# Fused attention and two feed-forward layers: which first-layer slices run inside attention, and how the decay table is loaded

## The chip, the cores and the metric

The kernel runs on one core of one Trainium2 chip. The metric is the device time of one execution in microseconds. The core has five engines that work from queues of their own and wait for each other by semaphores: TensorE (PE in the profile; PEld is its loading of weights), VectorE (DVE), ScalarE (ACT), GpSimd (POOL) and SyncE (SP), which here issues all DMA transfers.

## The reference

```
# q, k, v: [2 batches, 8 heads, 768 tokens, 64]; lam: one decay per head, 0.97 to 0.99
# per head, by blocks of 64 tokens:
intra = ((q_b k_b^T) * Dmask) v_b        # Dmask[i, j] = lam ** (i - j) for i >= j, else 0
inter = (q_b * lam ** (i + 1)) state
state = lam ** 64 * state + (k_b * lam ** (63 - j))^T v_b
x = heads side by side: [1536 tokens, 512]
h = x @ w_in                             # 512 -> 2048
x = act(h) @ w_out                       # act: 0 below -1, h above 1, (h + 1)**2 / 4 between
out = (sigmoid(x @ w_gate) * (x @ w_val)) @ w_out2     # 512 -> 1536 -> 512
```

## The kernel before

**Attention.** Blocks of 128 tokens are used instead of 64. There are 16 units, one for each batch, pair of heads and half of the tokens (384 tokens, three blocks). In the loop over units i, TensorE is given: the scores of unit i+1 (`scores`, L412), the state updates of unit i+1 (`updates`, L427), then the outputs of unit i (`outputs`, L475 from the weighed scores, L484 from the states). VectorE weighs the scores of i+1 with the decay table `DT` into `pT` (L442), builds the states `sc` (L451, L453), and writes the low part `xl` of unit i's output (L495); ScalarE copies the states (`st`, L465) and writes the high part `xh` (L494). GpSimd scales the keys of unit i+2 by the last column of `DT` (`pre_k`, L388, `kd`), and behind the outputs the queries of unit i+2 by the table `qp` (`pre_q`, L398, `qs`). SP loads unit i+4 into one of four buffers once unit i is done, then one weight piece.

**Numbers in two parts.** The feed-forward matmuls take each factor as a high part in the fast 32-bit format and a low part that holds the rest, so each product is three matmuls: high x high, low x high, high x low. The weights arrive as 64-bit floats in pieces of 512 columns (512 KB). A round (`w_round`) is a pipeline step over three pieces: `w_float` on piece k-1 (L92 and L93 on VectorE, L95 on VectorE or GpSimd), `w_high` on piece k-2 (L99, ScalarE), `w_words` on piece k (L85, L86, ScalarE) and `w_low` on piece k-2 (L103, the subtraction that makes the low part). Piece k-2 is usable when round k is done. Pieces 0, 1, 3, 5 are the four hidden weights of the first group, pieces 2, 4, 6, 7 their projection weights.

**Feed-forward.** `feed_forward` is a generator over (layer, group, third of the tokens, f); a group has four f. Each entry makes one hidden slice of twelve matmuls 128x512 (two slices in the second layer), then `act1` or `act2` makes `r` from it (L173, L174 on ScalarE, L175 on VectorE), and one entry later `split` makes the high part `gh` (L165, ScalarE) and low part `gl` (L166, VectorE). `finish` takes the oldest split entry and does its projection, again twelve matmuls (L202), into four accumulator banks, which are copied out behind the fourth f. PSUM has eight banks in one pool: scores (two), updates, outputs, hidden slice and the four accumulators all take theirs from it.

**What runs where.** The attention loop takes `next(steps)` at units 7 to 15 but 13. Each step is a hidden slice, or a projection, for which the generator stops a second time inside attention. The first third of the tokens (512) is complete behind unit 7, the second behind unit 14. By the code's order the eight steps are: hidden 0, 1, 2, projection 0, hidden 3, projection 1, hidden 4 (the second third), projection 2. Weight rounds stand at units 1, 3 and 5 to 12, ten of them, with L95 and L103 on GpSimd. Behind attention, `rounds` is not empty, the generator runs to its end, and rounds are done wholly on VectorE and ScalarE.

**Tables.** Ahead of unit 0, `tables` builds the first two heads' part of `DT` on VectorE and GpSimd (L346, L349), the first pair's `qp` on ScalarE (L357) and a row of powers per head, `pw`, on ScalarE (L363). `pw` is stored to memory (`pd`, L365), and two loads of `qp` (L370) and one of `DT` for heads 2 to 7 (L375, 384 KB) read it back, shifted by one element per partition.

Of the kernel before, what the change touches and what calls it, by code (L numbers as in the profile page):

```python
# [10 lines left out]
AF = mybir.ActivationFunctionType  # L11
# [3 lines left out]
B, H, S, D = 2, 8, 768, 64  # L15
NT, DM = B * S, H * D
FF1, FF2 = 2048, 1536
P = 128
# [7 lines left out]
GF = 4  # L26
PADW = 64
CST = 4 + PADW + P
FFREE = (13,)
NQD = 2  # L30
NWP, NRAW = 14, 5

# [2 lines left out]
def fused_kernel(ctx: ExitStack, tc: tile.TileContext, qkv, qd, cst, w1, w2, out):  # L35
    nc = tc.nc
    pe, act, dve, pool, sp = nc.tensor, nc.scalar, nc.vector, nc.gpsimd, nc.sync
# [63 lines left out]
    def w_low(i, eng):  # L101
        r = tmps.pop(i)[1]
        eng.tensor_tensor(out=ws[i][:, 1], in0=r, in1=ws[i][:, 0].bitcast(F32), op=ALU.subtract)  # L103

    def w_round(eng=dve, between=None):
        k = prog["round"]
        if k - 2 >= len(pieces):
            return  # L110
        if k - 2 >= NWP and pieces[k - 2 - NWP][0] >= prog["done"]:
            return
        prog["round"] += 1
        if 0 <= k - 1 < len(pieces):
            w_float(k - 1, eng)
        if between:
            between()
        if 0 <= k - 2:
            w_high(k - 2)
        if k < len(pieces):  # L120
            while prog["loaded"] <= k:
                w_load()
            w_words(k)
        if 0 <= k - 2:
            w_low(k - 2, eng)
        if eng is dve:
            w_load()

# [102 lines left out]
    def feed_forward(rounds):  # L231
        LAG = 2
        behind = []
        fresh = None

        def split():
            (ph, g, t, f), a = fresh
            behind.append((fresh[0], parts(a, ph * NF1 + g * GF + f, t)))

        def finish():  # L240
            (ph, g, t, f), gs = behind.pop(0)
            project((ph, g, t, f), gs)
            if f == GF - 1:
                flush((ph, g, t, f))
            if t == NTT - 1:
                prog["done"] += 1
            return f == GF - 1

        for u in seq:
            ph, g, t, f = u  # L250
            n = ph * NF1 + g * GF + f
            hs = [hidden(n, t, 0)] + ([hidden(n, t, 512)] if ph else [])
            if fresh:
                split()
            fresh = u, (act2(*hs, n, t) if ph else act1(hs[0], n, t))
            yield u
            flushed = False
            if len(behind) == LAG:
                flushed = finish()
                if not rounds:  # L260
                    yield u
            if rounds:
                if ph:
                    w_round()
                    w_round()
                elif not flushed:
                    w_round()
        split()
        while behind:
            finish()  # L270

    rounds = []
    steps = feed_forward(rounds)


    with ExitStack() as actx:
# [6 lines left out]
        nu = len(units)  # L283
# [30 lines left out]
        def tables():  # L314

            cs = tp.tile([P, 512], F32, tag="r", bufs=3, name="cs")
            dm = [tp.tile([P, 512], F32, tag="r", bufs=3, name=f"dm{j}")[:, 0:2 * (PADW + P)]
                  .rearrange("p (h x) -> p h x", h=2) for j in range(2)]
            sp.dma_start(out=cs[:, 0:CST], in_=cst)
            for i in range(NQD):  # L320
                u_load(i)
                q_diag[i] = wp.tile([P, 2, 512], F32, tag="w", name=f"qd{i}").rearrange(
                    "p a b -> p (a b)")[:, 0:2 * UT].rearrange("p (c e t) -> p c e t", c=CU, e=2)
                u_part(i, 1, 1)
                for c in range(CU):
                    if c < 2 or i:
                        c1 = CU if c or i else 1
                        sp.dma_start(out=q_diag[i][:, c:c1], in_=qd[i][:, c:c1])
                    if i:
                        break  # L330
            for i in range(NQD):
                u_part(i, 2, 2)
            for i in range(NQD):
                u_part(i, 0, 1)
            for j in range(2):
                dve.memset(dm[j][:, :, 0:PADW], 0.0)
            dve.memset(half, 0.5)
            pool.memset(pw[:, 0:P - 1], 0.0)
            pool.memset(pw[:, P - 1:P], 1.0)
            pool.memset(st[0], 0.0)  # L340
            act.activation(st[1], st[0], AF.Copy)
            sq = [cs[:, 0:2]] + [cs[:, CST + 2 * k:CST + 2 * k + 2] for k in range(6)]
            for k in range(7):
                w = 1 << k
                if k:
                    pool.tensor_tensor(out=sq[k], in0=sq[k - 1], in1=sq[k - 1], op=ALU.mult)  # L346
                for h in range(2):
                    src = cs[:, 4:CST] if k == 0 else dm[k % 2][:, h]
                    dve.scalar_tensor_tensor(  # L349
                        out=DT[:, h] if k == 6 else dm[(k + 1) % 2][:, h, PADW:],  # L350
                        in0=src[:, PADW - w:PADW + P - w], scalar=sq[k][:, h:h + 1],
                        in1=src[:, PADW:], op0=ALU.mult, op1=ALU.add,
                    )
            act.activation(qp[:, 0, 0:1], cs[:, 3:4], AF.Copy)
            for k in range(7):
                w = 1 << k
                act.activation(qp[:, 0, w:2 * w], qp[:, 0, 0:w], AF.Copy,  # L357
                               scale=qp[:, 0, w - 1:w])

            act.activation(pw[:, P:P + 1], cs[0:H, 2:3], AF.Copy)  # L360
            for k in range(7):
                w = 1 << k
                act.activation(pw[:, P + w:P + 2 * w], pw[:, P:P + w], AF.Copy,  # L363
                               scale=pw[:, P + w - 1:P + w])
            sp.dma_start(out=pd, in_=pw)  # L365
            u_load(2)
            w_load()
            pdv = pd[:, :]
            for e in range(2):
                sp.dma_start(  # L370
                    out=qp[e * D:(e + 1) * D, 1:],
                    in_=bass.AP(pdv.tensor, pdv.offset + (2 + e) * 2 * P + P,
                                [[0, D], [4 * P, NP - 1], [1, P]]),
                )
            sp.dma_start(  # L375
                out=DT[:, 2:],
                in_=bass.AP(pdv.tensor, pdv.offset + 4 * P, [[1, P], [2 * P, H - 2], [1, P]]),
            )
            u_load(3)
            w_load()  # L380

# [118 lines left out]
        with tc.manual_schedule():  # L500
# [11 lines left out]
            for i in range(nu):  # L512
# [9 lines left out]
                    outputs(i)  # L522
                    evacuate(i)

                if i in (1, 3) or 5 <= i <= 12:
                    w_round(pool, finish)
                else:
                    finish()
                if i + 2 < nu:
                    pre_q(i + 2)  # L530
                u_load(i + 4)
                w_load()
                if i >= nu // 2 - 1 and i not in FFREE:
                    next(steps)


# [68 lines left out]
```

## Time and profile before

| | us |
|---|---|
| median of 3 runs | 637.87 |
| lowest and highest run | 637.09, 2779.6 |
| the profiled execution, device time | 638.09 |
| its span, first to last instruction | 636.3 |
| TensorE busy in the span | 614.8 (97%) |
| VectorE, ScalarE, GpSimd busy | 352.5, 287.2, 56.8 |
| mean granted TensorE clock, of full speed | 0.983 |

The span is what the trace covers; the device time lies 1.79 us above it. Busy shares are means over the whole run: GpSimd works only in the first 90 us, and TensorE's idle time lies almost wholly there too. A bracket behind a row of a timeline gives the idle time of the engine before it and what ended it. SPq and POOLq are the queues in which SP and GpSimd issue DMAs.

### The profile page before, as it was taken

What the parts mean: (1) busy time and instruction counts of PE and PEld (TensorE: products, weight loads), DVE (VectorE), ACT (ScalarE), POOL (GpSimd) and SP (SyncE); (2) the same over time, 40 slices, a digit from 0 to 9 for tenths busy, and PEclk for the clock granted to TensorE, in tenths of its full rate; (3) what the DMA queues carried; (4) which work ended last, traced back from release to release, by engine and by line L of the source; (5) the groups of instructions that cost most, each with busy time, mean ns of one, the idle gap of its engine ahead of it and who ended that gap; (6) DMA issues with size and microseconds to landing.
All of it is one profiled execution on the core that took longest, in us unless ns stands there. A gap on an engine that the chain in (4) does not pass through costs nothing.

```text
span 636.3 us, 7871 instructions
## 1 busy us (share of the span) xinstructions
PE 614.8 (97%) x3072; PEld 507.7 (80%) x3072; DVE 352.5 (55%) x612; ACT 287.2 (45%) x511; POOL 56.8 (9%) x62
## 2 busy tenths in 40 slices
PE   6779889999999999999999999999999999999997
PEld 5667668888888888888888888888888888888886
DVE  4485864655666666666776912157843167713132
ACT  5356745665565556556675612144721145311110
POOL 3486740000000000000000000000000000000000
PEclk9789979999999999999999999999999999999999
DMA  8985520322132223122213400024420022001011
GB/s 262 349 291 220 199 66 1 101 66 67 66 100 66 67 67 91 56 60 92 66 34 99 133 0 1 1 66 133 132 67 0 1 59 74 1 1 67 0 67 66
DMA packets 16229, 53.37 MB, mean 84 GB/s; under 512 B 1720, under 2 KB 3648, under 8 KB 16192
## 3 DMA queue, kind: packets, MB, share of 16 engines
q1 hardware_dynamic: 16192, 52.87, 25.5%
q8 instruction: 24, 0.39, 0.3%
q14 instruction: 13, 0.11, 0.0%
HBM read 49.71 MB, written 3.15 MB: 83 GB/s over the span
## 4 chain that ended last, share of the span: by engine, by line
PE 88%; ACT 4%; DVE 4%; DMA 2%; issue 1%; POOL 1%; SPq 0%; POOLq 0%; ACTq 0%; DVEq 0%
PE a L202 35%; PE h L147 17%; PE h L148 17%; PE h L149 17%; DVE pT L442 1%; DMA DT<-pd 1%; PE x L484 1%; PE x L475 1%; ACT xh L494 1%; ACT st L465 1%; PE s L412 1%; DVE sc L453 1%; DMA pd<-pw 1%; DVE r L175 0%; DVE part L216 0%
## 5 line engine op out<-in xcount | busy, mean ns | idle before, releaser
L147 PE MATMUL h<-xh,w 128*128 128x512 f32 x480 | 188.3, 392 | 0.0
L148 PE MATMUL h<-xh,w 128*128 128x512 f32 x480 | 187.7, 391 | 0.0
L149 PE MATMUL h<-xl,w 128*128 128x512 f32 x480 | 187.3, 390 | 0.0
L202 PE MATMUL a<-gh,w 128*128 128x512 f32 x384 | 118.7, 390 | 0.5 <-DVE r L175 0.5
L148 PEld LDWEIGHTS h<-xh,w 128*128 128x128 f32 x480 | 90.7, 189 | 19.0 <-POOL w L103 0.3
L149 PEld LDWEIGHTS h<-xl,w 128*128 128x128 f32 x480 | 90.6, 189 | 18.9
L147 PEld LDWEIGHTS h<-xh,w 128*128 128x128 f32 x480 | 90.7, 189 | 18.6
L181 DVE TENSOR_TENSOR r<-r,h 128x512 f32<-128x512 f32 x36 | 24.7, 687 | 139.4 <-PE h L149 137.1
L202 PE MATMUL a<-w,gh 128*128 128x512 f32 x288 | 88.6, 389 | 0.0
L202 PEld LDWEIGHTS a<-gh,w 128*128 128x128 f32 x384 | 71.8, 188 | 15.5 <-DVE r L175 0.9
L175 DVE SCALAR_TENSOR_TENSOR r<-r,h 128x512 f32<-128x512 f32 x48 | 33.0, 687 | 87.1 <-ACT r L174 87.0
L165 ACT ACTIVATE gh<-r 128x512 fp32r<-128x512 f32 x84 | 52.4, 624 | 60.8 <-DVE r L181 55.5
L202 PE MATMUL a<-gl,w 128*128 128x512 f32 x192 | 74.7, 389 | 0.0
L173 ACT ACTIVATE r<-h,half 128x512 f32<-128x512 f32 x48 | 33.0, 688 | 91.5 <-PE h L149 91.5
L166 DVE TENSOR_TENSOR gl<-r,gh 128x512 fp32r<-128x512 f32 x84 | 58.4, 695 | 16.5 <-ACT gh L165 16.4
L202 PEld LDWEIGHTS a<-w,gh 128*128 128x128 f32 x288 | 54.1, 188 | 11.2
L180 ACT ACTIVATE r<-h 128x512 f32<-128x512 f32 x36 | 21.5, 597 | 87.2 <-PE h L149 87.2
L99 ACT ACTIVATE w<-wr 128x512 fp32r<-128x512 f32 x68 | 42.4, 623 | 39.6 <-DVE wr L95 39.2
L202 PE MATMUL a<-w,gl 128*128 128x512 f32 x144 | 56.0, 389 | 0.0
L93 DVE SCALAR_TENSOR_TENSOR wr<-raw,wr 128x512 uint32<-128x512 uint32 x68 | 50.1, 737 | 2.3
L85 ACT ACTIVATE wr<-raw 128x512 f32<-128x512 f32 x68 | 45.1, 664 | 0.8 <-POOL w L103 0.8
L86 ACT ACTIVATE wc<-raw 128x512 int32<-128x512 uint32 x68 | 44.8, 658 | 0.0
(51 smaller groups left out, 513.5 us busy)
## 6 DMA issues: line engine op xcount, KB each, us to landing
raw<-in_w SPq DMA_DIRECT2D x68, 512.0 KB, 3.6
u<-in_qkv SPq DMA_DIRECT2D x14, 768.0 KB, 5.7
out<-part SPq DMA_DIRECT2D x12, 256.0 KB, 2.1
u<-in_qkv SPq DMA_DIRECT2D x4, 192.0 KB, 5.6
u<-in_qkv SPq DMA_DIRECT2D x2, 384.0 KB, 6.2
qd<-in_qd SPq DMA_DIRECT2D x1, 384.0 KB, 5.4
DT<-pd SPq DMA_DIRECT2D x1, 384.0 KB, 6.3
qd<-in_qd SPq DMA_DIRECT2D x1, 256.0 KB, 3.7
```

Source lines behind the costliest of these rows:

```text
L85: act.activation(r, hi.bitcast(F32), AF.Copy, scale=2.0 ** -112)
L86: act.activation(c, lo, AF.Copy, scale=2.0 ** -29)
L93: dve.scalar_tensor_tensor(out=ru, in0=hi, scalar=0x80000000, in1=ru, op0=ALU.bitwise_and, op1=ALU.bitwise_or)
L99: act.activation(ws[i][:, 0], tmps[i][1], AF.Copy)
L147: pe.matmul(h, lhsT=wh, rhs=xh[:, k, tt], start=(k == 0), stop=False)
L148: pe.matmul(h, lhsT=wl, rhs=xh[:, k, tt], start=False, stop=False)
L149: pe.matmul(h, lhsT=wh, rhs=xl[:, k, tt], start=False, stop=(k == NP - 1))
L165: act.activation(gh, g, AF.Copy)
L166: dve.tensor_tensor(out=gl, in0=g, in1=gh.bitcast(F32), op=ALU.subtract)
L173: act.activation(r, h, AF.Relu, bias=half, scale=0.5)
L175: dve.scalar_tensor_tensor(out=r, in0=r, scalar=1.0, in1=h, op0=ALU.min, op1=ALU.max)
L202: pe.matmul(accs[j], lhsT=a, rhs=b_, start=(f == 0 and m == 0), stop=(f == GF - 1 and m == 2))
```

## The change

Four things are changed. First, inside attention only hidden slices are made, one each behind units 7, 9, 11 and 13; no projection runs there. To allow that, `finish` waits until three entries are split while attention runs (`LAG + 1`), and the generator no longer stops behind a projection. Behind attention the lag is two, as before, and a `while` does two projections at once at the first step there. Each projection is followed by its weight rounds as before. Second, the ten weight rounds stand at units 1, 3, 5, 6, 7, 8, 10, 12, 14 and 15. Third, in rounds at units below 8 the low-part subtraction (L103) runs on VectorE and no longer on GpSimd; there are three such subtractions, at units 5, 6 and 7 (the first two rounds have none). Fourth, in `tables` ScalarE makes `pw` first and stores it, then `qp`; the `DT` reload is cut into heads 2 and 3 and heads 4 to 7; the first weight load moves behind both.

```diff
--- before.py
+++ after.py
@@ -26,7 +26,8 @@
 GF = 4
 PADW = 64
 CST = 4 + PADW + P
-FFREE = (13,)
+HIDDEN = (7, 9, 11, 13)
+ROUNDS = (1, 3, 5, 6, 7, 8, 10, 12, 14, 15)
 NQD = 2
 NWP, NRAW = 14, 5
 
@@ -104,7 +105,7 @@
 
 
 
-    def w_round(eng=dve, between=None):
+    def w_round(eng=dve, between=None, low=dve):
         k = prog["round"]
         if k - 2 >= len(pieces):
             return
@@ -122,7 +123,7 @@
                 w_load()
             w_words(k)
         if 0 <= k - 2:
-            w_low(k - 2, eng)
+            w_low(k - 2, low)
         if eng is dve:
             w_load()
 
@@ -254,12 +255,8 @@
                 split()
             fresh = u, (act2(*hs, n, t) if ph else act1(hs[0], n, t))
             yield u
-            flushed = False
-            if len(behind) == LAG:
+            while len(behind) >= (LAG if rounds else LAG + 1):
                 flushed = finish()
-                if not rounds:
-                    yield u
-            if rounds:
                 if ph:
                     w_round()
                     w_round()
@@ -339,6 +336,18 @@
             pool.memset(pw[:, P - 1:P], 1.0)
             pool.memset(st[0], 0.0)
             act.activation(st[1], st[0], AF.Copy)
+
+            act.activation(pw[:, P:P + 1], cs[0:H, 2:3], AF.Copy)
+            for k in range(7):
+                w = 1 << k
+                act.activation(pw[:, P + w:P + 2 * w], pw[:, P:P + w], AF.Copy,
+                               scale=pw[:, P + w - 1:P + w])
+            sp.dma_start(out=pd, in_=pw)
+            act.activation(qp[:, 0, 0:1], cs[:, 3:4], AF.Copy)
+            for k in range(7):
+                w = 1 << k
+                act.activation(qp[:, 0, w:2 * w], qp[:, 0, 0:w], AF.Copy,
+                               scale=qp[:, 0, w - 1:w])
             sq = [cs[:, 0:2]] + [cs[:, CST + 2 * k:CST + 2 * k + 2] for k in range(6)]
             for k in range(7):
                 w = 1 << k
@@ -351,20 +360,7 @@
                         in0=src[:, PADW - w:PADW + P - w], scalar=sq[k][:, h:h + 1],
                         in1=src[:, PADW:], op0=ALU.mult, op1=ALU.add,
                     )
-            act.activation(qp[:, 0, 0:1], cs[:, 3:4], AF.Copy)
-            for k in range(7):
-                w = 1 << k
-                act.activation(qp[:, 0, w:2 * w], qp[:, 0, 0:w], AF.Copy,
-                               scale=qp[:, 0, w - 1:w])
-
-            act.activation(pw[:, P:P + 1], cs[0:H, 2:3], AF.Copy)
-            for k in range(7):
-                w = 1 << k
-                act.activation(pw[:, P + w:P + 2 * w], pw[:, P:P + w], AF.Copy,
-                               scale=pw[:, P + w - 1:P + w])
-            sp.dma_start(out=pd, in_=pw)
             u_load(2)
-            w_load()
             pdv = pd[:, :]
             for e in range(2):
                 sp.dma_start(
@@ -372,10 +368,13 @@
                     in_=bass.AP(pdv.tensor, pdv.offset + (2 + e) * 2 * P + P,
                                 [[0, D], [4 * P, NP - 1], [1, P]]),
                 )
-            sp.dma_start(
-                out=DT[:, 2:],
-                in_=bass.AP(pdv.tensor, pdv.offset + 4 * P, [[1, P], [2 * P, H - 2], [1, P]]),
-            )
+            for h0, h1 in ((2, 4), (4, H)):
+                sp.dma_start(
+                    out=DT[:, h0:h1],
+                    in_=bass.AP(pdv.tensor, pdv.offset + h0 * 2 * P,
+                                [[1, P], [2 * P, h1 - h0], [1, P]]),
+                )
+            w_load()
             u_load(3)
             w_load()
 
@@ -522,15 +521,15 @@
                     outputs(i)
                     evacuate(i)
 
-                if i in (1, 3) or 5 <= i <= 12:
-                    w_round(pool, finish)
+                if i in ROUNDS:
+                    w_round(pool, finish, pool if i >= nu // 2 else dve)
                 else:
                     finish()
                 if i + 2 < nu:
                     pre_q(i + 2)
                 u_load(i + 4)
                 w_load()
-                if i >= nu // 2 - 1 and i not in FFREE:
+                if i in HIDDEN:
                     next(steps)
```

## Rows read from the trace of the kernel before

**Rows 1.** Stretches: from:to, length, five engines' busy us (instructions), TensorE clock, DMA share, GB/s

```profile
7.50:27.50 20.00, 15.32 (x140) 12.91 (x139) 7.26 (x20) 5.45 (x14) 8.60 (x10) 0.83 0.97 342
27.50:40.00 12.50, 10.65 (x155) 8.93 (x153) 10.16 (x27) 6.87 (x16) 8.35 (x9) 1.00 0.90 307
40.00:50.00 10.00, 7.80 (x52) 6.38 (x48) 6.48 (x11) 5.72 (x12) 10.00 (x10) 0.66 0.85 304
50.00:100.00 50.00, 45.82 (x379) 36.19 (x378) 33.22 (x63) 28.29 (x55) 27.64 (x24) 0.93 0.39 138
100.00:632.00 532.00, 532.00 (x2349) 440.63 (x2347) 290.10 (x474) 234.53 (x399) 0.00 (x0) 1.00 0.18 57
```

**Rows 2.** Chain that ended last: start, length, what; one slice behind attention

```profile
101.96 2.72 PE a L202 x12
```

**Rows 3.** Timeline of TensorE in attention: start us, length, engine, line, what

```profile
50.17 0.94 PE L412 MATMUL s<-u 64*128 64x128 f32 x12
...
55.46 0.94 PE L412 MATMUL s<-u 64*128 64x128 f32 x12
...
58.17 0.47 PE L147 MATMUL h<-xh,w 128*128 128x512 f32 x1
...
96.23 0.70 PE L202 MATMUL a<-gh,w 128*128 128x512 f32 x2
```

**Rows 4.** Timeline of the first 21 us, several engines; in brackets idle time before

```profile
2.92 2.36 ACT L357 ACTIVATE qp<-qp 128x1 f32<-128x1 f32 x7
...
3.53 2.35 SPq L296 DMA_DIRECT2D u<-in_qkv  x4
...
5.41 2.35 ACT L363 ACTIVATE pw<-pw 8x1 f32<-8x1 f32 x7
...
7.84 0.34 SPq L365 DMA_DIRECT2D pd<-pw  x1
...
12.71 0.60 SPq L375 DMA_DIRECT2D DT<-pd  x1
...
19.13 0.56 DVE L442 TENSOR_TENSOR pT<-s,DT 128x384 f32<-128x384 f32 x1 [2.46 <-DMA DT<-pd]
...
20.09 0.91 PE L427 MATMUL uu<-u,kd 128*64 128x64 f32 x12 [3.99 <-POOL kd L388]
```

**Rows 5.** Timeline of 39 to 48 us, around unit 8, several engines

```profile
39.00 1.28 POOL L103 TENSOR_TENSOR w<-wr,w 128x512 fp32r<-128x512 f32 x1
...
39.58 0.94 PE L412 MATMUL s<-u 64*128 64x128 f32 x12 [0.76 <-DMA u<-in_qkv]
...
40.60 1.36 DVE L93 SCALAR_TENSOR_TENSOR wr<-raw,wr 128x512 uint32<-128x512 uint32 x1
...
42.71 0.91 PE L427 MATMUL uu<-u,kd 128*64 128x64 f32 x12 [2.20 <-POOL kd L388]
...
47.04 0.56 DVE L495 TENSOR_TENSOR xl<-x,xh 128x384 fp32r<-128x384 f32 x1 [0.24 <-ACT xh L494]
```

**Rows 6.** Chain that ended last, 58 to 66 us, steps of one unit

```profile
58.41 0.69 DVE r L175
...
61.98 0.63 ACT w L99
...
63.76 0.52 ACT gh L165
...
64.28 0.58 ACT r L173
...
65.55 0.70 DVE r L175
```

**Rows 7.** Waits of TensorE up to 120 us: total us, times, longest

```profile
PE s L412 <- DVE pT L442: 2.1, 2, 1.1
```

**Rows 8.** Groups by line: busy us, mean ns | idle before; page, first 150 us

```profile
L93 DVE SCALAR_TENSOR_TENSOR wr<-raw,wr 128x512 uint32<-128x512 uint32 x68 | 50.1, 737 | 2.3
...
L103 DVE TENSOR_TENSOR w<-wr,w 128x512 fp32r<-128x512 f32 x7 | 5.0, 709 | 0.0
```

## Prediction

> **What bounds the kernel now.** I read the table of stretches first. From 100 to 632 us TensorE is busy for 532.00 of 532 us at full clock; before that it is busy 7.80 of 10 us between 40 and 50, at a granted clock of 0.66, and 45.82 of 50 us between 50 and 100, at 0.93 [rows 1]. So nothing behind attention can be hidden or gained, and only what happens up to about 100 us is open. The chain that ended last gives the price of the unit of work: twelve matmuls of 128x512, called a slice here, take 2.72 us when TensorE runs without a gap [rows 2]. The code has 48 first-layer hidden slices, 48 first-layer projections and 36 x 3 in the second layer, 204 in all. When the last attention matmuls make room for the next projection at 96.2 us [rows 3], seven slices are done (five hidden, two projected) and 197 are left: 96.2 + 197 x 2.72 = 632.0, and the span of 636.3 leaves a tail of 4.3 (the last accumulation and stores).
>
> That gives the formula for the changed kernel. It does four hidden slices inside attention, so 200 are left. With X for the moment when TensorE has issued its last attention matmul, span = X + 200 x 2.72 + 4.3 = X + 548.3. The profiled time is 638.09 for a span of 636.3, so the time is X + 550.1. The median of the runs is 637.87, and the difference of 0.2 does not matter here. **Break-even is X = 88.0**: three slices (8.2 us) go behind attention, so attention must end 8.2 us sooner to pay for them. Every slice that TensorE takes later costs exactly what it saved, unless attention was waiting for something other than TensorE.
>
> **Part by part: the tables.** ScalarE computes the powers `pw` before `qp` instead of behind it, so `pw` is ready one chain of 2.36 us sooner than at 7.76 [rows 4]. The store `pd` can't use all of it: SP issues loads until 5.88, so the store moves from 7.84 to 5.9 at best. Its landing may not move at all, since it stands in the queue behind the same loads: bounds 0 and 1.9. The `DT` reload, issued at 12.71, was waited for until 19.13 by the first weighing of the second head pair, and through the key scaling on GpSimd by the updates at 20.09, with TensorE idle for 3.99 us [rows 4]. Now one third of it comes first, and a weight load of 512 KB no longer stands ahead. I take a landing at 15.5, between 13.4 and 19.0, nearer the early end because two thirds of the bytes and one load are out of the way. The updates then start near 16.5, about 3.5 us sooner. What moves back: `qp` is ready at 7.8 instead of 5.3, hidden because GpSimd uses it from 11.3 on; if that cover were gone it would cost 2.5. In SP's queue the load of unit 3 comes some 1.0 later, behind one more issue of 0.6 and a weight load's; the same bytes stand ahead of it, so I cost it at nothing, at most 1.0.
>
> That gain does not last. The DMA share is 0.97 between 7.5 and 27.5 and 0.90 between 27.5 and 40 [rows 1]: 0.6 + 1.25 = 1.85 us of idle transfer time in all, and every byte has still to come. At 39.58 the scores of unit 8 waited for their own load [rows 5]. So at unit 8 the tables are worth between 0 and 1.85; I take 1.0.
>
> **Units 5 to 7: three low-part subtractions from GpSimd to VectorE.** GpSimd takes 1.28 for one at 39.00, and behind it stood the key scaling for which the updates of unit 8 waited until 42.71, TensorE idle for 2.20 [rows 5]. After these idle times TensorE was granted half its clock in the stretch from 40 to 50 [rows 1]. Without the subtraction, and 1.0 sooner, the updates start at 42.7 - 1.3 - 1.0 = 40.4; 1.85 for the rest of the unit at full clock (2.71 from 55.46 to 58.17 [rows 3], less the scores) and one slice of 2.73 end at 45.0. That is TensorE's bound for the end of the first hidden slice, now just before 50.17 [rows 3]. VectorE has another: that slice's last matmul needs `xl` of unit 7, ready at 47.6 now [rows 5]. Two subtractions at 0.71 [rows 8] come before it (49.0); the shift takes 1.0, and a GpSimd that is less busy gives back about two times 0.6 (L93 took 1.36 at 40.60 against a mean of 0.74 [rows 5, 8]), and its idle time ahead of that `xl`, 0.24 and some before it, fills up. I take 45.9 for `xl` and 46.2 for the end of the slice: between 45.0 and 49.3 (no shift, nothing given back), by VectorE because it ends last. The first slice's `r` on VectorE then starts at 47.6, since relu and square take 1.4 [rows 6].
>
> **Units 8 to 15.** In the kernel before, each of units 7 to 12 had a weight round and a slice or projection. From 58.41 to 65.55 the chain goes through ScalarE and VectorE, not TensorE: 7.14 a unit, of which 1.78 is the round's work on ScalarE (L99, L85, L86) between the evacuation and the split [rows 6]. Now a unit with a slice alternates with one with a round. TensorE needs 58.17 - 50.17 = 8.00 for such a pair [rows 3]. The chain from one `r` to the next loses the 1.78 (ScalarE does it in the other unit, while VectorE weighs) and gains one unit's weighing (two at 0.56 [rows 4] and two state steps, 1.4), the round's L92 and L93 (1.15) and one `xl` (0.5): 7.14 - 1.78 + 3.05 = 8.4. I take 8.5 a pair, between 8.0 (TensorE) and 9.6 (both round operations doubled, as L93 was). So `r` of the second and third slice start at 56.1 and 64.6.
>
> The fourth slice, at unit 13, meets a new wait. Its weight piece is finished in the round of unit 12, on GpSimd. Counted from the third `r`: `r` 0.6, weighing 1.4, L92 and L93 1.15, then two GpSimd operations of 1.28 [rows 5] give 5.9 with the handover; TensorE could have started at 3.85. Everything on TensorE queues behind this second matmul of the slice. The slice ends at 8.65 and its `r` starts at 10.1 instead of 8.5: 74.7. The last weighing and the last outputs take 3.6 more (0.6, 1.4, 0.1, and 1.5 of matmuls): **X = 78.3**. Without the stall it is 76.7.
>
> The four accumulator banks that the projections held are free, so the 2.1 us in which scores waited for `pT` to release a bank [rows 7] go, with the slow clock after them. This is inside the pair count already. Behind attention two whole projections (5.4 us) cover the last evacuation and the fourth slice's split; the rounds there run with TensorE full, as now, so I cost the lag of three at nothing. If that cover failed it would show as TensorE idle behind X, at most one ScalarE-VectorE chain of some 3 us.
>
> **Sum.** 78.3 + 550.1 = 628.4 us, 9.7 below the profiled run, 1.5%.
>
> **Rivals.** A: TensorE itself is the bound of each pair and the fourth weight piece comes in time. 45.0 + 1.4 + 3 x 8.0 + 3.6 = 74.0, or 624.1; with the full 1.85 of the tables 623.3. For it: the chain of 8.4 is only just above 8.0. Against it: the piece of unit 12 has three operations in a row ahead of it. Chance 0.16.
>
> B: VectorE and GpSimd hold each other up, and the stall at the fourth slice lowers the clock. L93 went from 0.74 to 1.36 beside a working GpSimd [rows 5, 8]; three subtractions prolonged by 0.6 each give 1.8, and a slice and a unit partly at the lower of the two clock levels give 2.5, as the stretch from 40 to 50 did after idle times of the same size [rows 1, 5]. 628.4 + 1.8 to 4.3 = 630.2 to 632.7, to 634.5 with the pairs at 9.0. Chance 0.22. The Trainium skill (SBUF — State Buffer, Who interferes with whom) states the rule that speaks against the change: a VectorE instruction with two SBUF inputs and a GpSimd instruction that reads SBUF lock each other out, and the later one blocks wholly. The subtraction is of that kind; by that rule it could wait for a whole GpSimd operation. The trace's 1.36 agrees in kind.
>
> C, on the other side: the rounds and the attention chain, not the slices, set the pace, and units 8 to 15 keep their average, (96.2 - 50.2) / 8 = 5.75 us. Then X = 46.2 + 8 x 5.75 = 92.2 and the time 642.3, slower than before. It decides from 5.2 us a unit. For it: the chain ran through ScalarE and VectorE. Against it: that chain contained the 1.78 only because slice and round fell in one unit, and the bank waits belong to the projections. Chance 0.08.
>
> That the tables change does nothing at all is in the sum's bounds: 1.0 later, 629.4.
>
> **How the numbers follow.** The forecast's own range is 626 to 631, chance 0.50; A 0.16, B 0.22, C 0.08, and 0.04 lies outside them all. The range 623.5 to 634.5 holds the forecast, nearly all of B and most of A. Two per cent, about what a measurement of this kernel can tell from no change, is 12.8 us: faster means below 625.1, which is most of A (0.13); slower means above 650.6, which only several failures give (0.02); 0.85 lies between.
>
> **What would show it.** The updates of unit 2 start near 16.5, not 20.09; unit 8's scores near 38.5; no half clock between 40 and 50. The first slice ends near 46, the `r` of the four slices come 8.5 apart with a longer last step, TensorE waits about 2 us for L103 on GpSimd in the fourth slice, and the last attention matmul ends near 78. Behind it, 200 slices at 2.72 without a gap. The prediction is wrong if VectorE's chain gives pairs over 9.6, if the clock falls more than once behind 40 us, or if TensorE is idle behind X.

## The result, and the profile after

The changed kernel takes 630.57 us in the median (629.64 to 631.58, 4 runs) against 637.48 for the kernel before on the same chip: a ratio of 0.9894, 95% interval 0.9872 to 0.9917, 1.1% faster. The ratio leaves out one run of the kernel before, of 2779.6 us. The profiled execution took 631.58 us with a span of 629.8, the slowest of the four. On another occasion six runs gave 630.84 (629.05 to 631.61), ratio 0.9904.

Lines behind the changed places are shifted by up to one in the new kernel: L203 is the projection, L148 to L150 the hidden slice, L411 the scores, L426 the updates, L441 the weighing, L474 and L483 the outputs, L104 the low-part subtraction, L96 the round's addition on GpSimd, L176 the `r`.

The chain that ended last, behind attention. It answers [rows 2]; columns are start, length and what.

```profile
100.63 2.72 PE a L203 x12
```

A slice still costs 2.72 us. TensorE took up its first projection with ten of its matmuls behind the last outputs at 81.77, two of them having slipped in ahead: X = 81.3. The formula gives 81.3 + 548.3 = 629.6 for a span of 629.8. So attention ended 14.9 us sooner than 96.2 and gave 8.2 of it back as three slices.

Stretches of the changed kernel, to be laid beside [rows 1]: from:to, length, busy us of the five engines with their instructions, granted clock, DMA share, GB/s.

```profile
40.00:50.00 10.00, 6.86 (x66) 5.31 (x68) 8.57 (x17) 6.77 (x14) 7.70 (x8) 0.96 0.77 288
...
49.00:53.00 4.00, 4.00 (x40) 3.33 (x38) 2.73 (x8) 1.87 (x6) 1.73 (x2) 0.57 0.18 53
```

Between 40 and 49 there is no low clock in this execution (0.66 over 40 to 50 before). It came once, from 49 to 53, at 0.57. In the other profiled execution of the same kernel, of 630.69 us, it is the other way round: full clock from 49 to 53, and half clock from 42 to 44.

```profile
42.00:44.00 2.00, 2.00 (x16) 1.67 (x13) 1.90 (x3) 1.85 (x4) 1.66 (x2) 0.50 0.77 315
```

So the kernel does not fix where the clock falls, and the forecast of no half clock between 40 and 50 holds in one of two profiles, and there up to 49.

The start of the changed kernel, against [rows 4].

```profile
5.70 0.71 SPq L345 DMA_DIRECT2D pd<-pw  x1
...
12.05 1.33 SPq L366 DMA_DIRECT2D qp<-pd  x2
...
13.42 1.11 SPq L372 DMA_DIRECT2D DT<-pd  x2
...
18.17 0.56 DVE L441 TENSOR_TENSOR pT<-s,DT 128x384 f32<-128x384 f32 x1 [1.05 <-DMA DT<-pd]
...
19.13 0.91 PE L426 MATMUL uu<-u,kd 128*64 128x64 f32 x12 [2.50 <-POOL kd L387]
```

The store of `pw` was issued 2.1 us sooner than before (5.70 against 7.84), and what reads it back was issued 0.7 us later (12.05 against 11.33): SP waited 5.1 us for the store to land, 2.2 before. The updates of unit 2 came at 19.13, 0.96 sooner.

Units 7 and 8, against [rows 5]: scores and updates of unit 8, a subtraction of the change beside GpSimd's addition, then what the first slice waited for.

```profile
38.81 0.94 PE L411 MATMUL s<-u 64*128 64x128 f32 x12
...
41.46 0.57 PE L426 MATMUL uu<-u,kd 128*64 128x64 f32 x12 [1.71 <-POOL kd L387]
...
42.56 1.29 POOL L96 TENSOR_TENSOR wr<-wr,wc 128x512 int32<-128x512 int32 x1 [1.15 <-DVE wr L94]
...
43.01 1.39 DVE L104 TENSOR_TENSOR w<-wr,w 128x512 fp32r<-128x512 f32 x1
...
46.76 0.49 ACT L493 ACTIVATE xh<-x 128x384 fp32r<-128x384 f32 x1
...
47.31 0.50 PE L148 MATMUL h<-xh,w 128*128 128x512 f32 x1 [1.68 <-ACT xh L493]
```

The `r` operations of the four slices and the last outputs.

```profile
50.30 0.69 DVE L176 SCALAR_TENSOR_TENSOR r<-r,h 128x512 f32<-128x512 f32 x1 [1.23 <-ACT r L175]
...
59.51 0.69 DVE L176 SCALAR_TENSOR_TENSOR r<-r,h 128x512 f32<-128x512 f32 x1 [1.15 <-ACT r L175]
...
68.06 0.69 DVE L176 SCALAR_TENSOR_TENSOR r<-r,h 128x512 f32<-128x512 f32 x1 [0.46 <-ACT r L175]
...
78.04 0.69 DVE L176 SCALAR_TENSOR_TENSOR r<-r,h 128x512 f32<-128x512 f32 x1 [1.94 <-ACT r L175]
...
81.07 0.94 PE L483 MATMUL x<-qs,st 128*128 128x128 f32 x6
```

The steps are 9.21, 8.55 and 9.98 us; in the other profiled execution 8.55, 8.54 and 9.98. What TensorE waited for up to 120 us, for the lines that concern the change (total us, times, longest):

```profile
PE h L148 <- ACT xh L493: 1.7, 1, 1.7
...
PE h L149 <- POOL w L104: 1.4, 1, 1.4
```

The waits of the scores for a bank [rows 7] are gone. In their place are 1.7 for `xh` in the first slice and 1.4 for L104 in the fourth.

### The profile page after: what moved, and what is told of

Read it like the earlier page. It is cut to its first block, busy times and chain, and to the rows that moved or that the text cites. A ratio compares the mean times of both kernels' runs of the same rounds, so it can differ in the third digit from the quotient of the medians.

```text
span 629.8 us, 7890 instructions
## 1 busy us (share of the span) xinstructions
PE 611.0 (97%) x3072; PEld 504.9 (80%) x3072; DVE 354.5 (56%) x615; ACT 287.8 (46%) x511; POOL 51.6 (8%) x59
## 4 chain that ended last, share of the span: by engine, by line
PE 90%; DVE 4%; ACT 2%; DMA 2%; issue 1%; SPq 1%; POOL 0%; POOLq 0%; ACTq 0%
PE a L203 36%; PE h L149 17%; PE h L150 17%; PE h L148 17%; DVE pT L441 1%; DMA pd<-pw 1%; DMA DT<-pd 1%; PE x L483 1%; PE x L474 1%; DVE sc L452 1%; ACT st L464 1%; ACT xh L493 1%; PE s L411 1%; DVE w L104 0%; SPq L293 0%
## 5 line engine op out<-in xcount | busy, mean ns | idle before, releaser
L148 PE MATMUL h<-xh,w 128*128 128x512 f32 x480 | 187.4, 390 | 1.9 <-ACT xh L493 1.7
L150 PE MATMUL h<-xl,w 128*128 128x512 f32 x480 | 187.1, 390 | 0.0
L203 PE MATMUL a<-gh,w 128*128 128x512 f32 x384 | 118.4, 390 | 0.0
L148 PEld LDWEIGHTS h<-xh,w 128*128 128x128 f32 x480 | 90.2, 188 | 21.0 <-ACT xh L493 2.1
L150 PEld LDWEIGHTS h<-xl,w 128*128 128x128 f32 x480 | 90.1, 188 | 18.8 <-DVE xl L494 0.3
L203 PE MATMUL a<-w,gh 128*128 128x512 f32 x288 | 88.7, 389 | 0.0
L203 PEld LDWEIGHTS a<-gh,w 128*128 128x128 f32 x384 | 72.0, 188 | 14.9 <-issue 0.2
L176 DVE SCALAR_TENSOR_TENSOR r<-r,h 128x512 f32<-128x512 f32 x48 | 33.0, 688 | 82.3 <-ACT r L175 82.3
L203 PE MATMUL a<-gl,w 128*128 128x512 f32 x192 | 74.8, 390 | 0.0
L203 PEld LDWEIGHTS a<-w,gh 128*128 128x128 f32 x288 | 54.1, 188 | 11.2
L203 PE MATMUL a<-w,gl 128*128 128x512 f32 x144 | 56.1, 389 | 0.0
L94 DVE SCALAR_TENSOR_TENSOR wr<-raw,wr 128x512 uint32<-128x512 uint32 x68 | 49.6, 729 | 2.3
L104 DVE TENSOR_TENSOR w<-wr,w 128x512 fp32r<-128x512 f32 x63 | 45.1, 716 | 0.3
```

The costliest lines, as they stand in the source:

```text
L94: dve.scalar_tensor_tensor(out=ru, in0=hi, scalar=0x80000000, in1=ru, op0=ALU.bitwise_and, op1=ALU.bitwise_or)
L148: pe.matmul(h, lhsT=wh, rhs=xh[:, k, tt], start=(k == 0), stop=False)
L150: pe.matmul(h, lhsT=wh, rhs=xl[:, k, tt], start=False, stop=(k == NP - 1))
L176: dve.scalar_tensor_tensor(out=r, in0=r, scalar=1.0, in1=h, op0=ALU.min, op1=ALU.max)
L203: pe.matmul(accs[j], lhsT=a, rhs=b_, start=(f == 0 and m == 0), stop=(f == GF - 1 and m == 2))
```

## Experiments

Each kernel was timed in five rounds beside the kernel before; a ratio is to that kernel, and "the changed kernel" is the one above.

### The tables alone

The kernel before, with the fourth part of the change only.

```diff
+            act.activation(pw[:, P:P + 1], cs[0:H, 2:3], AF.Copy)
...
+            sp.dma_start(out=pd, in_=pw)
+            act.activation(qp[:, 0, 0:1], cs[:, 3:4], AF.Copy)
...
-            sp.dma_start(out=pd, in_=pw)
             u_load(2)
-            w_load()
...
-                out=DT[:, 2:],
...
+            for h0, h1 in ((2, 4), (4, H)):
...
+                    out=DT[:, h0:h1],
...
+            w_load()
```

> The kernel before with the tables part alone: pw before qp, the DT reload in two parts, the first weight load behind them. Theory (the gain at unit 2 is swallowed by transfers that are busy all the time up to unit 8): updates of unit 2 start about 1 us sooner, as in the changed kernel (19.1 against 20.1), but the updates of unit 8 move by less than 1 us from 42.7, and the time falls by 0 to 1.0 us. Rival (waiting for the reload was a real part of what attention lost): everything behind moves by the same amount and the time falls by 2 us or more.

636.55 us against 636.78, ratio 1.0002 (0.9988 to 1.0016). The updates of units 2 and 8:

```profile
18.57 0.91 PE L429 MATMUL uu<-u,kd 128*64 128x64 f32 x12 [2.41 <-POOL kd L390]
...
42.14 0.91 PE L429 MATMUL uu<-u,kd 128*64 128x64 f32 x12 [2.95 <-POOL kd L390]
```

Unit 2 gained 1.5 us (20.09 before), unit 8 0.6 (42.71 before), and the time nothing. One profile each says little here: over all profiles the updates of unit 2 start at 19.25 to 20.09 with the old tables (four kernels) and at 18.14 to 19.21 with the new (ten), and the scores of unit 8, where the rounds ahead of it are the same, at 37.33 to 39.58 (four) and 38.25 to 38.95 (eight). So the gain at unit 2 is there and is gone at unit 8. The theory holds; that attention waits for other transfers in between is argued from the DMA share [rows 1].

### The slices alone

The kernel before, with the first part of the change only.

```diff
-FFREE = (13,)
+HIDDEN = (7, 9, 11, 13)
...
-            if len(behind) == LAG:
+            while len(behind) >= (LAG if rounds else LAG + 1):
                 flushed = finish()
-                if not rounds:
-                    yield u
-            if rounds:
...
-                if i >= nu // 2 - 1 and i not in FFREE:
+                if i in HIDDEN:
                     next(steps)
```

> The kernel before with the slices alone: four hidden slices at units 7, 9, 11, 13, no projection in attention, lag of three there; rounds at their old units, low parts on GpSimd, old tables. Theory (a unit with both a slice and a round costs the ScalarE-VectorE chain of 7.1 us, and a GpSimd round in every unit about 4.4, so the slices alone gain little): attention ends between 84 and 88, the time falls by 0 to 4 us. Rival (the slices and the freed banks are the whole gain, where the rounds stand is worth nothing): the time falls by 5.5 us or more, to within 1.5 us of the changed kernel.

640.20 us, ratio 1.0063 (1.0044 to 1.0082): **slower** than before. Both expectations were wrong. GpSimd's queue from the end of unit 8 to the start of unit 10, and the updates of unit 12, which waited for it:

```profile
57.43 1.18 POOL L394 TENSOR_TENSOR qs<-u,qp 128x384 f32<-128x384 f32 x1
...
58.57 1.29 POOL L384 TENSOR_TENSOR kd<-u,DT 128x384 f32<-128x384 f32 x1
...
59.82 1.28 POOL L95 TENSOR_TENSOR wr<-wr,wc 128x512 int32<-128x512 int32 x1
...
61.05 1.73 POOL L103 TENSOR_TENSOR w<-wr,w 128x512 fp32r<-128x512 f32 x1
...
62.74 0.99 POOL L394 TENSOR_TENSOR qs<-u,qp 128x384 f32<-128x384 f32 x1
...
63.70 1.02 POOL L384 TENSOR_TENSOR kd<-u,DT 128x384 f32<-128x384 f32 x1
...
64.77 0.57 PE L423 MATMUL uu<-u,kd 128*64 128x64 f32 x12 [2.23 <-POOL kd L384]
```

Scalings and rounds follow each other without a gap, two scalings and two round operations a unit, 5.3 us from one query scaling to the next (57.43 to 62.74). The updates wait for the last of these, 2.23 us. The `r` operations (the third, at 72.59, is left out), a subtraction on VectorE ahead of the fourth, and all that TensorE waited for from 46 to 100 us:

```profile
51.34 0.69 DVE L175 SCALAR_TENSOR_TENSOR r<-r,h 128x512 f32<-128x512 f32 x1 [4.20 <-ACT r L174]
...
61.57 0.68 DVE L175 SCALAR_TENSOR_TENSOR r<-r,h 128x512 f32<-128x512 f32 x1
...
81.62 1.48 DVE L103 TENSOR_TENSOR w<-wr,w 128x512 fp32r<-128x512 f32 x1
...
85.15 0.68 DVE L175 SCALAR_TENSOR_TENSOR r<-r,h 128x512 f32<-128x512 f32 x1
...
PE uu L423 <- POOL kd L384: 4.1, 4, 2.2
PE x L471 <- DVE pT L438: 3.4, 1, 3.4
```

The steps are 10.2, 11.0 and 12.6 us for two units. From 46 us on TensorE waits 4.1 us for the key scaling, in the kernel before not at all. In the third step the chain that ended last runs through VectorE: a round done wholly there (L95, then L103 at 81.62) stands ahead of the fourth `r`, and TensorE waits 3.4 us for the last weighing. By the prediction's formula attention ended at 639.5 - 548.3 = 91.2, 5.0 us sooner than 96.2, and three slices cost 8.2. That is rival C's result (92.2), by queues that the prediction had not summed for it.

### The spread rounds alone

The kernel before, with the rounds moved as far as its eight steps allow.

```diff
-                if i in (1, 3) or 5 <= i <= 12:
+                if i in (1, 3, 5, 6, 7, 8, 10, 11, 12, 14):
```

> The kernel before with the rounds spread as far as its own eight slice and projection steps allow (units 1, 3, 5, 6, 7, 8, 10, 11, 12, 14 instead of 1, 3, 5 to 12), nothing else changed. Theory (spreading the rounds pays only where units without a slice take them, and here every unit from 7 on but 13 has one): the time is within 2 us of the kernel before. Rival (the rounds' spacing alone is the gain): it falls by 5 us or more.

636.83 us, ratio 1.0003 (0.9989 to 1.0016). Spreading the rounds alone gives nothing, as the theory said. It is a weaker test than the others: one round moves (from unit 9 to 14), where the change moves two (from 9 and 11 to 14 and 15).

### Slices and spread rounds, without tables and low parts

The edit is to the kernel with the slices alone.

```diff
-                if i in (1, 3) or 5 <= i <= 12:
+                if i in (1, 3, 5, 6, 7, 8, 10, 12, 14, 15):
```

> The kernel before with the slices and the spread rounds alone: low parts of the first half on GpSimd, old tables in the old order. Theory (the gain is that a unit has either a slice or a round; tables and low parts are worth nothing): within 1.2 us of the changed kernel. Rival (tables and low parts, worth nothing alone, are needed beside the slices): 2 us or more above the changed kernel.

630.62 us, ratio 0.9908 (0.9884 to 0.9933), beside 630.84 (0.9904) for the changed kernel on the same chip:

> The changed kernel once more, on the same chip and beside the same runs of the kernel before as the other three, as their measure. Both theories: 629.5 to 632, 1% below the kernel before. Its runs should spread by about 2 us, since one fall of the clock in attention is worth 1.5 to 3 us and some executions have one more than others.

So two of the four parts are the whole gain, as far as these intervals tell, and they are it together: slices +0.6%, rounds 0, both -0.9%. In the profile of the two parts TensorE waits 0.3 us for the key scaling from 46 us on (4.1 with the slices alone) and not at all for the last weighing, and the `r` are 8.54, 8.55 and 9.97 apart.

The spread of the changed kernel's runs is 2.6 us here; the kernel before spreads more (634.42 to 638.62). What makes one execution slower than the next was not traced run by run, and one rival is open: part of the gain may be falls of the clock that come less often. Over all experiments the runs of the kernel before at a mean clock of 0.991 or 0.992 took 634.42 to 636.71 us (10 runs), those at a lower one 635.66 to 638.70 (35); the changed kernel at 0.991 or 0.992 took 629.64 to 631.58 (7), and at 0.995 or 0.996 no less (629.05 to 631.61, 3). At the clock that both have the difference is about 4 us and not 6. No run separates this.

### Low parts of units 5 to 7 back on GpSimd

```diff
-                    w_round(pool, finish, pool if i >= nu // 2 else dve)
+                    w_round(pool, finish, pool)
```

> The changed kernel with the three low-part subtractions at units 5 to 7 back on GpSimd. Theory (it was a trade: on VectorE they took 1.1 to 1.5 us each instead of 0.7 and stood on the path to the first slice; on GpSimd they make the key scaling of unit 8 late by 1.3 and TensorE idle longer): within 1.5 us of the changed kernel. Rival A (VectorE was the wrong place): the first r starts 2 to 3 us sooner and the time falls by 2 to 3. Rival B (the clock): TensorE idles over 2 us before the updates of unit 8, the granted clock falls between 40 and 50, and the time rises by 2.5 to 4.

630.24 us, ratio 0.9914 (0.9893 to 0.9934), as the theory said. The scores and the updates of unit 8 and the first `r` in its profiled run:

```profile
38.49 0.94 PE L411 MATMUL s<-u 64*128 64x128 f32 x12
...
41.66 0.57 PE L426 MATMUL uu<-u,kd 128*64 128x64 f32 x12 [2.24 <-POOL kd L387]
...
48.24 0.69 DVE L176 SCALAR_TENSOR_TENSOR r<-r,h 128x512 f32<-128x512 f32 x1 [1.98 <-ACT r L175]
```

From the start of the scores the updates took 3.17 us to come, in the changed kernel 2.65; from the updates to the first `r` it took 6.58, there 8.84. So the trade can be seen: on VectorE the subtractions let the updates come sooner, on GpSimd they leave the way to the `r` shorter. Which is better one profile can't tell. In this one the first `r` came 2.06 sooner (48.24 against 50.30), as rival A said. But the last kernel below has the same code up to unit 12, and in its profile the updates came 3.91 behind the scores, the clock was at 0.50 from 44 to 46, as rival B said of it, and the first `r` came at 50.63. Four more profiles with the subtractions on VectorE have it at 49.22 to 50.10, always 8.83 to 8.85 behind the updates. By the times this part of the change is worth nothing that five rounds can tell.

### Low part of unit 12 on VectorE

```diff
-                    w_round(pool, finish, pool if i >= nu // 2 else dve)
+                    w_round(pool, finish, pool if i >= nu // 2 and i != 12 else dve)
```

> The changed kernel with the low-part subtraction of unit 12 on VectorE instead of GpSimd, so that the fourth slice does not wait for two GpSimd operations in a row. Theory: the wait of 1.4 us in that slice is gone, VectorE's chain gets 0.5 to 0.7 longer there, and the step between the third and the fourth r falls from 10.0 to about 9.3: the time falls by 0.5 to 1.0 us. Rival (the chain through VectorE takes over the whole wait): the step stays at 9.8 to 10.2 and the time is the same within 0.4.

630.27 us, ratio 0.9902 (0.9884 to 0.9921). The wait in the fourth slice and the third and fourth `r`:

```profile
PE h L149 <- DVE w L104: 0.7, 1, 0.7
...
67.19 0.69 DVE L176 SCALAR_TENSOR_TENSOR r<-r,h 128x512 f32<-128x512 f32 x1 [0.47 <-ACT r L175]
...
77.02 0.69 DVE L176 SCALAR_TENSOR_TENSOR r<-r,h 128x512 f32<-128x512 f32 x1 [0.55 <-ACT r L175]
```

The wait fell from 1.4 to 0.7, but the step stayed at 9.83 (9.98). The rival holds: the chain that ended last goes through L104 on VectorE there (1.18 us at 71.06), the weighing, the state copies and ScalarE's work on the slice, and no longer through TensorE.

### Early rounds

```diff
-ROUNDS = (1, 3, 5, 6, 7, 8, 10, 12, 14, 15)
+ROUNDS = (1, 2, 3, 4, 5, 8, 10, 12, 14, 15)
...
-                w_load()
+                if i not in (3, 4):
+                    w_load()
```

> The changed kernel with the rounds of units 6 and 7 moved to units 2 and 4, where attention waits for its transfers (rounds at 1, 2, 3, 4, 5, 8, 10, 12, 14, 15); the weight loads at units 3 and 4 are left out so that the transfers keep their order. Theory (VectorE and ScalarE work of the rounds stands on the path to the first slice, and ahead of unit 6 there is idle time for it): the first r starts at 46 to 48 instead of 50.3 and the time falls by 2 to 4 us against the changed kernel. Rival (VectorE is already busy for 11.1 of 12.5 us between 27.5 and 40, so the rounds only push attention back there): the first r starts at 49.5 or later and the time is within 1 us of the changed kernel or above it.

633.37 us, ratio 0.9939 (0.9923 to 0.9954), worse than the changed kernel's 0.9894 and 0.9904. A subtraction at unit 3 and the updates of units 6, 7 and 8:

```profile
31.01 1.59 DVE L104 TENSOR_TENSOR w<-wr,w 128x512 fp32r<-128x512 f32 x1
...
34.31 0.57 PE L426 MATMUL uu<-u,kd 128*64 128x64 f32 x12 [0.97 <-POOL kd L387]
...
38.95 0.45 PE L426 MATMUL uu<-u,kd 128*64 128x64 f32 x8 [1.68 <-POOL kd L387]
...
43.59 0.91 PE L426 MATMUL uu<-u,kd 128*64 128x64 f32 x12 [2.02 <-POOL kd L387]
```

The three updates are 4.6 us apart, each waiting for GpSimd; in the changed kernel they came at 34.24, 37.13 and 41.46. The first `r` came at 51.24. The subtraction takes 1.59 instead of 0.71 [rows 8]. The rival holds: there was no room ahead of unit 6 for more rounds. With their low parts on GpSimd:

> As the kernel with early rounds, with the three low-part subtractions of the first half (units 3, 4, 5) on GpSimd instead of VectorE. Theory: VectorE is the fuller engine there; the first r starts within 1 us of 46 to 47 and the time is 0 to 1.5 us below that of the kernel with early rounds. Rival (GpSimd then needs 4.4 us a unit and the key scaling is late): the updates of units 5 to 7 wait for it and the time is 1 us or more above.

633.42 us, ratio 0.9937 (0.9921 to 0.9954), the same. The first `r` came at 51.34. The updates of units 6, 7 and 8 wait for GpSimd, 2.47, 0.57 and 1.59 us, as the rival said, but the time is not above that of the kernel with early rounds. Neither expectation holds whole.

### Three slices in attention

```diff
-HIDDEN = (7, 9, 11, 13)
+HIDDEN = (7, 9, 11)
```

> The changed kernel with three slices in attention (units 7, 9, 11) instead of four, so that 201 are left behind it. By span = X + 2.72 x slices left + 4.3, one slice more costs 2.72. Theory (the fourth slice's step of 10.0 us contains a wait of 1.4 and a chain that units without a slice don't have): units 12 and 13 without it take 5.5 to 6.5, attention ends 3.5 to 4.5 us sooner, and the time falls by 0.8 to 1.8. Rival (the slice fills time that TensorE would have idled anyway): attention ends less than 2.7 us sooner and the time rises by 0 to 2.7.

633.11 us, ratio 0.9932 (0.9916 to 0.9949): 0.28 to 0.38% of 637 above the two ratios of the changed kernel, 1.8 to 2.4 us, for the one slice of 2.72. The rival holds. In the trace: GpSimd behind the round of unit 12, the updates of unit 15, the clock after that, the last outputs.

```profile
69.51 1.28 POOL L96 TENSOR_TENSOR wr<-wr,wc 128x512 int32<-128x512 int32 x1 [2.02 <-ACT xh L493]
...
70.75 1.27 POOL L104 TENSOR_TENSOR w<-wr,w 128x512 fp32r<-128x512 f32 x1
...
71.97 1.00 POOL L397 TENSOR_TENSOR qs<-u,qp 128x384 f32<-128x384 f32 x1
...
72.92 0.85 POOL L387 TENSOR_TENSOR kd<-u,DT 128x384 f32<-128x384 f32 x1
...
73.82 0.69 PE L426 MATMUL uu<-u,kd 128*64 128x64 f32 x8 [2.98 <-POOL kd L387]
...
73.00:80.00 7.00, 6.18 (x38) 4.55 (x39) 4.74 (x10) 2.85 (x6) 4.28 (x4) 0.51 0.23 75
...
80.24 0.94 PE L483 MATMUL x<-qs,st 128*128 128x128 f32 x6
```

Four GpSimd operations in a row, 4.3 us, stand ahead of the updates. TensorE, without its slice, waits 2.98 and is then at 0.51 of its clock from 73 to 80. Its last outputs start at 80.24, in the two profiles of the changed kernel at 81.07 and 80.19. With the slice, the same GpSimd time lies beside matmuls. By these profiles the slice is nearly free there.

### The first projection at unit 14, and what is left

```diff
-HIDDEN = (7, 9, 11, 13)
+HIDDEN = (7, 9, 11, 13, 14)
...
                 flushed = finish()
+                if not rounds:
+                    yield u
                 if ph:
```

> The changed kernel with the first projection at the end of unit 14, ahead of the last outputs, instead of behind attention. It fills the time in which TensorE waits for the last weighing (about 1 us between 79.2 and 81.0). Theory (TensorE's idle time there is the only thing left at the end): 0.5 to 1.0 us below the changed kernel. Rival (the accumulators' four banks, taken one unit sooner, or the later last outputs hold something up): the same or above.

629.93 us, ratio 0.9891 (0.9869 to 0.9914), beside 0.9904 for the changed kernel. TensorE at the end of attention:

```profile
77.59 0.70 PE L203 MATMUL a<-gh,w 128*128 128x512 f32 x2
...
80.53 0.88 PE L476 MATMUL x<-pT,u 128*64 128x128 f32 x12
```

The projection runs from 77.59 to the last outputs at 80.53. The difference of 0.9 us in the medians is of the size expected, but the intervals overlap: it is not shown. With that, the low part of unit 12 on VectorE and those of units 5 to 7 on GpSimd:

```diff
-                    w_round(pool, finish, pool if i >= nu // 2 else dve)
+                    w_round(pool, finish, dve if i == 12 else pool)
```

> The changed kernel with the first projection at unit 14, the low part of unit 12 on VectorE and those of units 5 to 7 on GpSimd. Theory: the first r near 48.2 as with the low parts on GpSimd, the fourth slice without its wait of 1.4, the end filled: 1 to 3 us below the changed kernel, 628 to 629.5. Rival (each step only moves the wait to the next engine): within 1 us of the changed kernel.

628.43 us (628.33 to 629.88, 5 runs), ratio 0.9876 (0.9853 to 0.9899), 2.4 us below the changed kernel on the same chip and the fastest of all kernels here; against the changed kernel the intervals still touch. The updates of unit 8 and the first `r`:

```profile
42.86 0.91 PE L428 MATMUL uu<-u,kd 128*64 128x64 f32 x12 [2.97 <-POOL kd L389]
...
50.63 0.69 DVE L176 SCALAR_TENSOR_TENSOR r<-r,h 128x512 f32<-128x512 f32 x1 [3.04 <-ACT r L175]
```

In this execution, its slowest, TensorE waited 2.97 us for the updates, and the first `r` came at 50.63, no sooner than in the changed kernel, and not at 48.2. So the profile does not show where the gain of its faster runs lies, and that stays open.

## Why the prediction was right, point by point

**The price of a slice and the break-even: right.** 2.72 a slice, X + 548.3 and X = 81.3 give the measured span within 0.2, and one slice less in attention cost 1.8 to 2.4 us of 2.72 where X fell by less than 1.

**The tables: mechanism right, size off.** The updates of unit 2 were put at 16.5 and came at 19.13. The term that was mis-sized is the landing of the reload, 15.5 in the text, 18.1 by the weighing at 18.17. Of the bounds for the store, the lower one, 0, was true: issued 2.1 us sooner, it was read back no sooner (12.05 against 11.33; over all profiles 10.98 to 12.05 with the new order and 10.70 to 12.08 with the old). Why it landed no sooner is not shown. The two `qp` loads still stood ahead of the reload, and the reload took 4.7 us from its issue though it was a third as large (6.3 before). The allowance for unit 8 was right in kind: what unit 2 gained was gone there, and the time gained nothing.

**Units 5 to 7: the term that failed.** Scores of unit 8 at 38.5 (38.81), updates at 40.4 (41.46), end of the first slice 46.2 (48.4), first `r` 47.6 (50.30). This 2.7 is nearly all of the 3.0 by which X was missed. About 1.1 of it lies ahead of the updates, and that changes from one execution to the next (40.38 to 41.46 in five profiles of the same code). The rest is the way from the updates to the `r`: 7.2 in the forecast, 8.84 in all five, within 0.01, and with the subtractions on GpSimd 6.58 at full clock and 7.77 where the clock fell. So the mis-sized term is the subtraction on VectorE. The three took 1.51, 1.39 and 1.13 us beside GpSimd, not 0.71. That is the mechanism of rival B, though of the 1.9 us that they lost only the 1.5 of the first two lies ahead of the end of the first slice. What was set against them did come: the round's L94, 1.36 before (as L93), took 0.69 at 41.73 and at 46.40. The Trainium skill's rule (SBUF — State Buffer, Who interferes with whom) agrees: each subtraction ended 0.55 us behind the GpSimd addition that was running when it started (44.40 and 43.85 for the pair shown above), so what it lost is, but for 0.16, the rest of that operation.

The second miss is where the slice waited. It waited 1.68 us for `xh` at its tenth matmul; `xl`, which its last matmul needs, itself stood behind `xh`. The state copies stand ahead of `xh` on ScalarE, these wait for the states, the states stand behind the weighing, and the weighing stood behind the subtraction. The prediction followed VectorE's queue to `xl` and missed that it reaches `xh` sooner, through another engine. That the updates come sooner without the subtractions on GpSimd can be seen, but its size, put at 1.3, is not settled: counted from the scores they took 1.76 to 2.65 in the five profiles, and 3.17 and 3.91 in two with the subtractions on GpSimd.

**Units 8 to 15: right in size, not in every step.** Steps of 8.5, 8.5 and 10.1 were forecast, 9.21, 8.55 and 9.98 came. The first contains the low clock from 49 to 53; in the other profile of the same kernel, at full clock there, it is 8.55. The second step runs through the two weighings as written down, but between them through ScalarE's state copies and `xh` (61.55 to 62.70) and not through L93 and L94, for which 1.15 had been put; these ended 0.1 us sooner beside it. The third has the wait for L104, 1.4 instead of 2. That wait alone does not make the step long, as the prediction had it: halved, it left the step at 9.83. The end took 3.3 of the forecast 3.6.

**The argument for the pairs: right for the change, incomplete as a reason.** It said that a unit with a slice and one with a round share the ScalarE work of 1.78. The runs show two more queues: with the slices alone, from 46 us on, TensorE waits 4.1 us for GpSimd's key scaling and 3.4 for a weighing behind a round on VectorE, and with the rounds spread 0.3 and 0. The prediction followed GpSimd's queue for units 5 to 8 and 12 and did not sum it for a unit with both scalings and a round.

**The rivals.** A (624) did not come: the chain stayed above TensorE's 8.00. B came in part, 1.5 us of lock ahead of the first slice and in one of two profiles some 0.7 of low clock (a first step of 9.21 against 8.55), not at the fourth slice. C did not come for the change and did for its first part alone. The result of 630.57 lies in the forecast's own range of 626 to 631, but near its upper end, and in B's 630.2 to 632.7 as well; the sum was 628.4, and the profiled execution, 631.58, lies outside the range. That the median fell inside is in part luck.

## What to carry to other kernels

Work that is moved behind a full engine has a fixed price; what moves it earns must come from the engine that bounds the stage it leaves, so count every engine's queue in that stage for a unit with and without it. Two changes that each give nothing or a loss can be one gain, where the first leaves units free and the second puts into them what had crowded the others. A slice that fills an idle TensorE may be nearly free, and taking it out can leave the end of the stage where it was. And one profile of a kernel is one execution: where the clock falls in it may differ in the next, so lengths between two events of one chain say more than the times at which these stand.

## What the runs showed of the hardware

A store of 8 KB that was issued at 5.68 to 6.54 us was read back no sooner than one issued at 7.84 to 7.95: SP issued the first load of it at 10.98 to 12.05 against 10.70 to 12.08. A VectorE subtraction of 128x512 with both inputs in SBUF took 0.71 us alone. Issued while GpSimd did an addition, it ended 0.54 or 0.55 us behind the end of that addition, in all seven cases (three in the changed kernel, three with early rounds, one at unit 12; 1.10 to 1.59 us each), and the GpSimd scaling behind it took 1.44 to 1.47 us and not 1.00. TensorE's clock was at the lower of its two levels for some us after a wait of 2.98 (0.51 from 73 to 80 in the kernel with three slices), after one of 1.68 (0.57 from 49 to 53) and after one of 1.56 (0.50 from 42 to 44 in the other profile of the changed kernel). But waits of 1.67 to 1.70 at the same place in three other kernels, and one of 2.24 with the low parts on GpSimd, left it at 1.00. So the length of one wait does not tell whether the clock falls.
